# Maxima over partitions by a diagonal product in the attention part, and index tables made on VectorE

## The chip, the cores and the metric

The kernel runs on one core of a Trainium2 chip. The metric is the device time of one execution in microseconds (us). Three runs of the kernel before gave 1014.26, 1008.35 and 1012.25 us, so the median is 1012.25 us. The engines are PE (TensorE: matmuls, and PEld for its weight loads), DVE (VectorE), ACT (ScalarE), POOL (GpSimd) and SP, whose queue issues most DMAs.

## The reference

Three stages follow each other. Attention with 32 memory slots per head (4 batches, 8 heads, 576 tokens, 64 columns) gives x of 2304 tokens by 512 columns; a mixture of 8 experts, two per token, works on x; a second feed-forward of width 2048 with clipped gates gives the output.

```python
a = softmax(phi over the sequence)                 # [b, h, s, 32]
k_m, v_m = a^T k, a^T v                            # [b, h, 32, 64]
attn = softmax(q k_m^T / 8);  x = attn v_m         # [2304, 512]
logits = x @ w_gate + log1p(exp(x @ w_noise)) * noise
# top 2 experts e per token, softmax weights over the two
out[token] += weight * (relu(x[token] @ w1[e]) @ w2[e])
h = out @ w_in;  result = (h * clip(h + 3, 0, 6) / 6) @ w_out
```

## The kernel before

Attention is done in 8 groups of 4 heads (two groups make a batch; each of the 6 token columns holds 96 tokens on partitions). Per group the loads are phi (288 KB), q, k and v (576 KB each). The stages are: transposes of phi and its softmax (`stage_a1`, L502 to L516), transposes of q (`stage_q`, L524 to L534), the products with k and v (L554) and what follows from them (`stage_a2`, L560 to L587), the scores and their softmax (`stage_b`, L598 to L615, two of its steps on POOL: L604 and L613) and the product with the values (`stage_c`, L621 on POOL makes its operand `vb`, L640 is the product). After the second group of a batch its tokens are routed (`route`: some 40 small VectorE instructions and a few products).

From the routed tokens of the first batches, expert 0 starts while attention still runs (`early`: gather of token rows on POOL, L823; transposes on PE, L833; layer 1, L848; layer 2, L867). The rest of expert 0, experts 1 to 7 and the second feed-forward are part 2, in which other buffers are used.

Products in float16 need numbers within range, so several things are scaled by a power of two under their largest magnitude: per batch the values `v_m` (`us`), and each expert's w1 and w2 (`wam`). `scale_w` (L409 to L417) does that: a maximum along the row on VectorE gives one number per partition (`war`, L413), GpSimd's custom instruction PARTITION_ALL_REDUCE (L414) takes the maximum over the 128 partitions and gives it to all of them, and four small VectorE instructions make the scales (`wsm`, L416 and L389 to L394). For a batch the scale goes into `mp` (L587) and by L621 into `vb`. For weights, ScalarE and VectorE then split each of the four pieces into two halves (L403, L405); w2 of expert 0 is loaded into the same buffer as w1, once w1 is split (`st0`, one buffer, L426).

The order of all instructions is made beforehand by a planner (`Sched`): it lists every instruction with a duration, what it reads and writes and its due time, and each engine takes the one due first of those that it believes ready. On the chip each engine works through its list in that order and waits for what isn't ready. The planner counts 0.45 us for L414. Part 1 (attention and early expert 0) and part 2 are planned one behind the other.

Before the first stage constants are made: 34 warm-up products on PE, an identity matrix `ident` by `make_identity` on POOL (its second instruction, masks.py:199, is an AFFINE_SELECT), and index tables by IOTA on POOL (L316 to L325) that VectorE converts.

Of the kernel before, what the change touches and what calls it, by code (L numbers as in the profile page):

```python
# [12 lines left out]
BF16 = mybir.dt.bfloat16  # L13
# [9 lines left out]
PT = 96  # L23
# [7 lines left out]
BIG = 64  # L31
# [11 lines left out]
WARM = 34  # L43
CDMA = 1
# [3 lines left out]
def _atanh_coefs(n=5):  # L48
    """atanh(s) / s on 0 <= s <= 1/3 as a polynomial in s^2, to float32's last bit."""
# [9 lines left out]
class Buf:  # L59
    """One instance of a rotating tile, allocated when its first instruction is issued."""  # L60
# [28 lines left out]
class Sched:  # L89
    """Lists the instructions of a program with what they read and write, then issues them engine by  # L90
    engine in the order in which a list scheduler (earliest due first) would start them."""
# [71 lines left out]
    def first_due(self):  # L163
        """Latest times of all instructions if TensorE never waited."""
# [15 lines left out]
    def place(self, back):  # L180
        """List schedule by due time, from the program's start, or backwards from its end."""
# [95 lines left out]
def attn_moe_kernel(ctx, tc, q, k, v, phi, w_gate, w_noise, noise, w1, w2, w_in, w_out, out):  # L277
# [13 lines left out]
    # ---- constants  # L291
    onesh = const.tile([128, 128], F16, name="onesh")
    POOL.memset(onesh, 1.0)
    with tc.tile_pool(name="warm", bufs=1, space=bass.MemoryType.PSUM) as wp:
        pw = wp.tile([128, 128], F32, name="pw")
        for i in range(WARM):
            PE.matmul(pw, onesh, onesh, start=True, stop=True)
    ident = const.tile([128, 128], F32, name="ident")
    make_identity(nc, ident)
# [15 lines left out]
    jp = const.tile([PT, PT], I32, name="jp")  # L315
    POOL.iota(jp, pattern=[[1, PT]], base=0, channel_multiplier=-1)  # L316
    tri = const.tile([PT, PT], F16, name="tri")
    DVE.tensor_scalar(tri, jp, 0.0, None, op0=ALU.is_gt)
    toki = const.tile([PT, B * NJ], I32, name="toki")
    POOL.iota(toki.rearrange("p (b j) -> p b j", b=B), pattern=[[S, B], [1, NJ]], base=-NT // 2,  # L320
              channel_multiplier=NJ)
    tok = const.tile([PT, B * NJ], F32, name="tok")
    DVE.tensor_copy(tok, toki)
    ioi = const.tile([PT, 128], I32, name="ioi")
    POOL.iota(ioi, pattern=[[1, 128]], base=0, channel_multiplier=0)  # L325
    iof = const.tile([PT, 128], F32, name="iof")
    DVE.tensor_copy(iof, ioi)
    ef = iof[:, :NE]
    ioc = const.tile([PT, NE * NTI], F32, name="ioc")
    DVE.tensor_scalar(ioc, iof[:, :NE * NTI], float(BIG * NTI), None, op0=ALU.subtract)  # L330
    io12 = const.tile([PT, 128 + NE * NTI, 2 * NJ], F16, name="io12")
    POOL.tensor_copy(io12[:, :128], iof[:, :, None].to_broadcast([PT, 128, 2 * NJ]))
# [23 lines left out]
    # ---- tiles  # L356
# [4 lines left out]
    for pl, spec in (  # L361
            (psa, dict(da=3, oa=2)),
            (psb, dict(two=2, o3=3, o1=1)),
            (main, dict(wa=2, st0=1, xTr=1, xg=3, yt=2, wsm=6, war=2, wam=2)),
# [872 lines left out]
```

## Time and profile before

| what | us |
|---|---|
| runs, median (lowest to highest) | 1012.25 (1008.35 to 1014.26) |
| profiled execution, first to last instruction | 1015.7 |
| PE busy, share of the span | 905.2, 89% |
| DVE, ACT, POOL busy | 590.5, 452.5, 151.7 |

The profiled execution spans 1015.7 us; what lies around the span is not shown apart, so the span stands for its own time. It is 3.45 us (0.3%) above the median of the runs. In a row of a timeline the first two numbers are start and duration in us, then engine, line, operation, output and inputs with shapes; in square brackets is how long the engine was idle before it and what ended that. "issue" there means that the engine waited for nothing that the profile shows. PEclk is the granted clock of TensorE as a share of 2.4 GHz (0.5 is 1.2 GHz). A DMA share of 1 means that all 16 DMA engines were busy throughout.

### The profile page before, as it was taken

What the parts mean: (1) busy time and instruction counts of PE and PEld (TensorE: products, weight loads), DVE (VectorE), ACT (ScalarE), POOL (GpSimd) and SP (SyncE); (2) the same over time, 40 slices, a digit from 0 to 9 for tenths busy, and PEclk for the clock granted to TensorE, in tenths of its full rate; (3) what the DMA queues carried; (4) which work ended last, traced back from release to release, by engine and by line L of the source; (5) the groups of instructions that cost most, each with busy time, mean ns of one, the idle gap of its engine ahead of it and who ended that gap; (6) DMA issues with size and microseconds to landing.
All of it is one profiled execution on the core that took longest, in us unless ns stands there. A gap on an engine that the chain in (4) does not pass through costs nothing.

```text
span 1015.7 us, 14429 instructions
## 1 busy us (share of the span) xinstructions
PE 905.2 (89%) x5659; PEld 527.5 (52%) x5659; DVE 590.5 (58%) x1073; ACT 452.5 (45%) x681; POOL 151.7 (15%) x188
## 2 busy tenths in 40 slices
PE   5557447997999999898999998999999999999996
PEld 4345235564555564545565554555555555555553
DVE  1566448737979494856858536786436354343332
ACT  3365354547756273735555446544323242222322
POOL 2223233221210202020000013442001000000000
PEclk6787678997999999998999999999999999999999
DMA  9993222377997959495866423534031030200101
GB/s 227 210 253 94 52 69 85 91 279 218 293 302 233 254 169 246 169 267 160 250 227 218 151 103 113 112 99 115 10 59 43 1 71 1 52 11 2 32 1 33
DMA packets 116217, 136.45 MB, mean 134 GB/s; under 512 B 54576, under 2 KB 83248, under 8 KB 116144
## 3 DMA queue, kind: packets, MB, share of 16 engines
q1 hardware_dynamic: 109872, 115.54, 40.5%
q0 software_dynamic: 6272, 19.93, 7.4%
q8 instruction: 46, 0.75, 0.3%
q14 instruction: 27, 0.22, 0.1%
HBM read 95.26 MB, written 28.39 MB: 122 GB/s over the span
## 4 chain that ended last, share of the span: by engine, by line
PE 54%; DVE 13%; issue 11%; DMA 6%; ACT 6%; POOL 2%; SPq 1%; POOLq 0%; DVEq 0%; ACTq 0%
PE two L953 16%; PE o L977 16%; PE two L848 11%; PE o L867 8%; DMA xT<-xg 2%; DVE wa L405 2%; PE da L640 1%; DVE wb L405 1%; ACT wa L403 1%; DMA st<-moe_w_d 1%; DMA xg<-xf,ids 1%; ACT wb L403 1%; DMA ys<-yt 1%; DVE w64o L472 1%; DMA w<-moe_w_in_d 1%
## 5 line engine op out<-in xcount | busy, mean ns | idle before, releaser
L953 PE MATMUL two<-xT,wa 128*128 128x384 f16 x1152 | 196.4, 328 | 0.0
L977 PE MATMUL o<-wb,hh 128*128 128x512 f16 x864 | 194.6, 379 | 1.1 <-DVE hh L964 1.0
L953 PEld LDWEIGHTS <-wa 128*128 128x128 f16 x1152 | 113.2, 98 | 80.2 <-issue 1.7
L867 PEld LDWEIGHTS <-hh 128*128 128x128 f16 x888 | 86.7, 98 | 100.6 <-DVE hh L858 0.7
L977 PEld LDWEIGHTS <-hh 128*128 128x128 f16 x864 | 83.8, 98 | 98.4 <-DVE hh L964 2.9
L848 PE MATMUL two<-xT,wb 128*128 128x320 f16 x768 | 112.2, 308 | 8.5 <-ACT hh L856 7.6
L960 ACT ACTIVATE hf<-hf,c 128x768 f32<-128x768 f32 x48 | 44.8, 934 | 139.9 <-DVE hf L958 138.9
L867 PE MATMUL o<-wb,hh 128*128 128x512 f16 x480 | 105.9, 379 | 0.3 <-DVE hh L858 0.3
L848 PEld LDWEIGHTS <-wa 128*128 128x128 f16 x864 | 80.8, 98 | 37.2 <-issue 10.3
L958 DVE TENSOR_TENSOR hf<-two,ivb 128x768 f32<-128x768 f32 x48 | 45.8, 955 | 93.0 <-PE two L953 93.0
L848 PEld LDWEIGHTS <-wb 128*128 128x128 f16 x768 | 77.2, 101 | 43.2 <-issue 9.4
L867 PE MATMUL o<-wa,hh 128*128 128x512 f16 x408 | 90.3, 379 | 0.0
L848 PE MATMUL two<-xT,wa 128*128 128x320 f16 x576 | 80.5, 299 | 5.6 <-ACT hh L856 5.6
L640 PE MATMUL da<-vb,at 128*96 128x272 f32 x96 | 36.0, 531 | 49.2 <-POOL vb L621 25.9
L823 POOL DMA_INDIRECT xg<-xf,ids x40 | 43.7, 1092 | 199.1 <-DMA xT<-xg 171.6
L858 DVE TENSOR_TENSOR hh<-hf,hh 128x640 f16<-128x640 f32 (+1 forms) x64 | 49.2, 770 | 39.8 <-ACT hh L856 39.4
L855 ACT ACTIVATE hf<-two 128x640 f32<-128x640 f32 (+1 forms) x64 | 42.3, 661 | 60.2 <-PE two L848 60.1
L961 DVE SCALAR_TENSOR_TENSOR hh<-hf,two 128x768 f32<-128x768 f32 x48 | 45.7, 953 | 38.7 <-ACT hf L960 37.5
L964 DVE TENSOR_TENSOR hh<-hh,hh 128x768 f16<-128x768 f32 x48 | 45.9, 956 | 33.3 <-ACT hh L963 33.3
L963 ACT ACTIVATE hh<-hh 128x768 f16<-128x768 f32 x48 | 40.4, 841 | 44.4 <-DVE hh L961 44.4
L405 DVE SCALAR_TENSOR_TENSOR wb<-st,wsm,wb 128x1024 f16<-128x1024 f32 x40 | 49.4, 1281 | 7.4 <-ACT wb L403 7.3
L405 DVE SCALAR_TENSOR_TENSOR wa<-st,wsm,wa 128x1024 f16<-128x1024 f32 x40 | 49.7, 1279 | 2.9 <-ACT wa L403 2.8
(208 smaller groups left out, 1033.7 us busy)
## 6 DMA issues: line engine op xcount, KB each, us to landing
st<-moe_w_d SPq DMA_DIRECT2D x32, 1024.0 KB
ys<-yt SPq DMA_DIRECT2D x40, 256.0 KB
w<-moe_w_in_d SPq DMA_DIRECT2D x16, 512.0 KB
wf<-w64o SPq DMA_DIRECT2D x32, 256.0 KB
w<-moe_w_out_d SPq DMA_DIRECT2D x16, 512.0 KB
st<-wf SPq DMA_DIRECT2D x8, 1024.0 KB
kv<-k_d SPq DMA_DIRECT2D x8, 576.0 KB
kv<-v_d SPq DMA_DIRECT2D x8, 576.0 KB
```

The lines of the kernel that those rows point to most:

```text
L405: sch.op("DVE", dve(1024), lambda s=s, w=w, c=c: DVE.scalar_tensor_tensor(w.t[:, 1, c], s.t[:, c], sm.t[:, 2], w.t[:, 0, c], op0=ALU.mult, ...
L640: PE.matmul(po.t[:, j, :XC], at.t[:, c:c + PT], vb.t, start=True, stop=True)
L823: sch.op("POOL", 1.05, lambda t=t, xg=xg: POOL.indirect_dma_start(out=xg.t, out_offset=None, in_=xf[:rows], in_offset=bass.IndirectOffsetO ...
L848: PE.matmul(ph.t[:, i, :nw], wa.t[:, wi, c * 1024 + fb * 128:c * 1024 + fb * 128 + 128], xT.t[:, 4 * xi + c, i * nw:(i + 1) * nw], start=( ...
L858: sch.op("DVE", dve(n), lambda: DVE.tensor_tensor(hh.t[:, 1], hf.t, hh.t[:, 0], op=ALU.subtract), [hf, (hh, 0)], [(hh, 1)])
L867: PE.matmul(py.t, hs[fb].t[:, hi, tsl], wb.t[:, wi, fb * 512:(fb + 1) * 512], start=(fb == 0 and n == 0), stop=(fb == 7 and n == 2))
L953: PE.matmul(ph.t[:, i, :CW], win[fb // 8].t[:, wi, o:o + 128], xT.t[:, 4 * xi + kc, :CW], start=(n == 0), stop=(n == 11))
L958: sch.op("DVE", dve(768), lambda: DVE.tensor_tensor(t1.t, ph.t[:, :, :CW], ivb.t[:, None, :CW].to_broadcast([128, 2, CW]), op=ALU.mult), [ ...
L960: sch.op("ACT", act(768, ptr=1), lambda: ACT.activation(t1.t, t1.t, AF.Relu, bias=c3, scale=CG), [], [t1])
L961: sch.op("DVE", dve(768), lambda: DVE.scalar_tensor_tensor(gf.t, t1.t, 6.0 * CG, ph.t[:, :, :CW], op0=ALU.min, op1=ALU.mult), [t1, ph], [gf])
L964: sch.op("DVE", dve(768), lambda: DVE.tensor_tensor(g.t[:, 1], gf.t, g.t[:, 0], op=ALU.subtract), [gf, (g, 0)], [(g, 1)])
L977: PE.matmul(po[m_].t, g.t[:, gi, i, m_ * 128:(m_ + 1) * 128], wou[fb // 8].t[:, wi, (fb % 8) * 512:(fb % 8 + 1) * 512], start=(fb == 0 and ...
```

## The change

In part 1 (`sch.seg` is 0 there and 1 in part 2) `scale_w` no longer calls the custom instruction. It multiplies the identity by the column of maxima, which puts them on the diagonal of `wdg`; a product with a matrix of ones sums each column over the partitions, so that every partition holds all 128 maxima in a row of PSUM; a maximum along that row gives the same number everywhere. That holds for six calls: four batches and expert 0's w1 and w2. Part 2 keeps the custom instruction. The identity, the index tables and the token numbers are made by VectorE: a row of indices by doubling, its transpose for the partition's index, and comparisons.

```diff
+MAXPE = 0
+WLAT = (0.0, 3.0)
@@ constants
+    iof, iop, ioq = ...   # [128, 128], [128, 32], [128, 32] of float32
+    DVE.memset(iof[:, 0:1], 0.0)
+    for n in (1, 2, 4, 8, 16, 32, 64):
+        DVE.tensor_scalar(iof[:, n:2 * n], iof[:, :n], float(n), None, op0=ALU.add)
+    for i in range(4):
+        DVE.memset(ioq[32 * i:32 * i + 32], 32.0 * i)
+    DVE.transpose(iop, iof[:, :32])
+    DVE.tensor_tensor(iop, iop, ioq, op=ALU.add)
     ident = const.tile([128, 128], F32, name="ident")
-    make_identity(nc, ident)
+    DVE.tensor_scalar(ident, iof, iop[:, 0:1], None, op0=ALU.is_equal)
...
-    POOL.iota(jp, pattern=[[1, PT]], base=0, channel_multiplier=-1)
-    DVE.tensor_scalar(tri, jp, 0.0, None, op0=ALU.is_gt)
+    DVE.tensor_scalar(tri, iof[:PT, :PT], iop[:PT, 0:1], None, op0=ALU.is_gt)
-    POOL.iota(toki...); DVE.tensor_copy(tok, toki); POOL.iota(ioi...); DVE.tensor_copy(iof, ioi)
+    DVE.tensor_scalar(p6, iop[:PT, 0:1], float(NJ), float(-NT // 2), op0=ALU.mult, op1=ALU.add)
+    for b in range(B):
+        DVE.tensor_scalar(tok[:, b * NJ:(b + 1) * NJ], iof[:PT, :NJ], p6, float(S * b), op0=ALU.add, op1=ALU.add)
@@ def scale_w
+        if sch.seg <= MAXPE:
+            wd, px = new("wdg", [128, 128], BF16), new(PS[sch.seg][2], [128, 128])
+            sch.op("DVE", 0.15, lambda: DVE.tensor_scalar(wd.t, identb, ar.t[:, 0], None, op0=ALU.mult), [(ar, 0)], [wd],
+                   lat=WLAT[sch.seg])
+            sch.op("PE", 0.06, lambda: PE.matmul(px.t, onesb, wd.t, start=True, stop=True), [wd], [px], lat=0.12)
+            sch.op("DVE", dve(128), lambda: DVE.tensor_reduce(ar.t[:, 1], px.t, axis=AX.X, op=ALU.max), [px], [(ar, 1)])
+            pow2_ops(...)   # as before
+            return sm
         sch.op("POOL", 0.45, lambda: POOL.partition_all_reduce(...), [(ar, 0)], [(ar, 1)])
```

The planner makes its order anew, so instructions of part 1 change places; in part 2 nearly all stay. Three places show it. Lines of the changed kernel are 16 higher from L414 on (L613 is L629 there, L848 is L864).

On POOL, around the first batch's maximum (`war`), the order before was this; an ISA row stands where the engine's code is set for the instruction behind it:

```order
L604 TENSOR_TENSOR sc_352<-sc_352,sm_359 128x576
L414 ISA
L414 ISA war_382<-war_382 128x1
L613 ISA
L613 TENSOR_TENSOR sc_352<-sc_352,sm_359 128x576
L621 TENSOR_TENSOR vb_356<-kd_283,mp_455 128x256
L621 TENSOR_TENSOR vb_441<-kd_366,mp_455 128x256
```

and now it is this, from the first instruction of the softmax on:

```order
L620 ISA
L620 TENSOR_TENSOR sc_367<-sc_367,sm_370 128x576
L629 TENSOR_TENSOR sc_367<-sc_367,sm_370 128x576
L637 TENSOR_TENSOR vb_338<-kd_294,mp_474 128x256
L620 TENSOR_TENSOR sc_472<-sc_472,sm_476 128x576
L637 TENSOR_TENSOR vb_445<-kd_377,mp_474 128x256
```

The reduction and both settings of code around it are gone, and one setting stands ahead of the first softmax instead.

On VectorE, at the program's start, conversions of POOL's tables stood ahead of the first maximum of phi (`st`, from `da` in PSUM):

```order
L301 CAST identh<-ident 128x128
L303 CAST identb<-ident 128x128
L318 TENSOR_SCALAR tri<-jp 96x96
L323 CAST tok<-toki 96x24
L327 CAST iof<-ioi 96x128
L509 TENSOR_REDUCE st_216<-da_205 128x1
```

Now VectorE builds the tables (the first rows, with five doublings, are left out here):

```order
L306 TENSOR_SCALAR iof<-iof 128x32
L309 STREAM_TRANSPOSE iop<-iof 128x32
L306 TENSOR_SCALAR iof<-iof 128x64
L337 TENSOR_SCALAR ioc<-iof 96x40
L310 TENSOR_TENSOR iop<-iop,ioq 128x32
L312 TENSOR_SCALAR ident<-iof,iop 128x128
L329 TENSOR_SCALAR tri<-iof,iop 96x96
L314 CAST identh<-ident 128x128
```

The identity is VectorE's own fourteenth row and waits for no other engine.

On PE, where group 6's product with the values (`da` from `vb`) meets expert 0's early start, the last transpose of gathered tokens (`xg`), the product and layer 1 (with `wa`, w1's halves) followed each other:

```order
L833 LDWEIGHTS xg_1384
L833 MATMUL oa_1463<-identh,xg_1384 128x128
L640 MATMUL da_1473<-vb_1194,at_1445 96x272 x2
L848 LDWEIGHTS wa_1429
L848 MATMUL da_1492<-xTe_1456,wa_1429 128x256
```

Now w2's diagonal `wdg` has its product there:

```order
L656 MATMUL da_1459<-vb_1245,at_1454 96x272 x2
L656 MATMUL da_1464<-vb_1245,at_1454 96x272 x2
L656 MATMUL da_1494<-vb_1245,at_1454 96x272 x2
L426 LDWEIGHTS onesb
L426 MATMUL oa_1559<-wdg_1557,onesb 128x128
L849 LDWEIGHTS xg_1361
L849 MATMUL oa_1561<-identh,xg_1361 128x128
```

The product for w2's maximum stands ahead of all transposes of the gathered tokens and of layer 1; before, neither of them stood behind w2's maximum on PE.

## Rows read from the trace of the kernel before

**Rows 1.** Busy time by stretch, as the columns in the first row say.
```profile
core 0: us, PE busy (x) PEld busy (x) DVE busy (x) ACT busy (x) POOL busy (x), PEclk, DMA share, GB/s
...
30.00:45.00 15.00, 3.30 (x25) 2.17 (x26) 4.92 (x14) 3.21 (x6) 2.62 (x4) 0.68 1.08 243
...
80.00:103.00 23.00, 20.51 (x163) 14.88 (x162) 18.27 (x65) 14.55 (x30) 8.21 (x8) 0.78 0.31 86
103.00:119.00 16.00, 2.51 (x58) 1.78 (x54) 5.98 (x28) 2.01 (x4) 1.58 (x5) 0.63 0.27 63
...
156.00:208.00 52.00, 45.84 (x376) 32.07 (x376) 40.58 (x124) 28.38 (x66) 15.51 (x20) 0.94 0.31 100
208.00:1015.70 807.70, 773.57 (x4440) 432.06 (x4438) 473.30 (x696) 354.56 (x488) 91.88 (x96) 0.98 0.47 134
```

**Rows 2.** Waits up to 200 us: who, for whom; total, times, longest.
```profile
...
PEld da L640 <- POOL vb L621: 50.1, 4, 14.1
```

**Rows 3.** Timeline of POOL: start, duration, engine, line, tiles; idle time before.
```profile
...
11.04 0.28 POOL masks.py:199 TENSOR_SCALAR_AFFINE_SELECT ident<-ident 128x128 f32<-128x128 f32 x1 [9.82 <-issue]
...
35.20 0.41 POOL L414 PARTITION_ALL_REDUCE war<-war  x1 [6.19 <-issue]
42.79 1.15 POOL L613 TENSOR_TENSOR sc<-sc,sm 128x576 f32<-128x576 f32 x1 [7.19 <-issue]
43.91 1.41 POOL L621 TENSOR_TENSOR vb<-kd,mp 128x256 f32<-128x256 f32 x2
```

**Rows 4.** Timeline of PE: the matmuls behind its longest idle times.
```profile
...
11.37 1.22 PE L507 MATMUL da<-ident,phr 96*128 96x96 f32 x6 [6.57 <-POOL ident masks.py:199]
...
44.90 5.05 PE L640 MATMUL da<-vb,at 128*96 128x272 f32 x12 [11.22 <-DVE at L615]
...
79.53 3.90 PE L640 MATMUL da<-vb,at 128*96 128x272 f32 x8 [12.10 <-POOL vb L621]
...
119.33 2.12 PE L640 MATMUL da<-vb,at 128*96 128x272 f32 x4 [13.82 <-POOL vb L621]
...
155.77 3.91 PE L640 MATMUL da<-vb,at 128*96 128x272 f32 x8 [12.04 <-DVE at L615]
```

**Rows 5.** Timeline of DVE: the chains around the first three maxima.
```profile
...
28.36 0.29 DVE L568 TENSOR_REDUCE us<-kd 128x1 f32<-128x128 f32 x1
28.68 0.15 DVE L413 TENSOR_REDUCE war<-us 128x1 f32<-128x2 f32 x1
...
62.36 0.10 DVE L413 TENSOR_REDUCE war<-us 128x1 f32<-128x2 f32 x1
...
101.64 0.09 DVE L413 TENSOR_REDUCE war<-us 128x1 f32<-128x2 f32 x1
...
111.22 0.34 DVE L587 TENSOR_SCALAR mp<-maskp,wsm 128x256 f32<-128x256 f32 x1
```

**Rows 6.** Timeline of PE: the products of groups 2 and 3 that use k and v.
```profile
...
49.88 1.52 PE L554 MATMUL oa<-kv,e 96*32 96x128 f32 x48
...
58.76 1.52 PE L554 MATMUL oa<-kv,e 96*32 96x128 f32 x48
```

**Rows 7.** Expert 0: POOL, SP, DMA from 168 to 170 us, PE.
```profile
...
146.16 0.76 POOL L414 PARTITION_ALL_REDUCE war<-war  x2 [7.05 <-issue]
...
161.84 0.95 SPq L426 DMA_DIRECT2D st<-moe_w_d  x2
...
168.00:170.00 2.00, 2.00 (x27) 1.84 (x24) 1.97 (x6) 1.49 (x7) 0.39 (x1) 1.00 0.52 199
...
162.63 2.78 PE L848 MATMUL da<-xTe,wa 128*128 128x256 f16 x24 [0.48 <-ACT xv L646]
...
177.78 0.41 POOL L414 PARTITION_ALL_REDUCE war<-war  x1 [5.89 <-DVE hhe L858]
...
182.45 7.93 PE L867 MATMUL oa<-wa,hhe 128*128 128x512 f16 x36
```

**Rows 8.** One line of VectorE: duration ns min/median/max, first and last start.
```profile
...
L703 DVE SCALAR_TENSOR_TENSOR gt<-gt,iof x8: 196/204/1203, 85.2 to 192.3; 96x48 f32<-96x48 f32 x8
```

More of the change, by code (lines that the diff above doesn't have):

```diff
@@ L8 @@
 from concourse.bass import ds
-from concourse.masks import make_identity
 from concourse._compat import with_exitstack
@@ L297, in attn_moe_kernel @@
             PE.matmul(pw, onesh, onesh, start=True, stop=True)
+    iof = const.tile([128, 128], F32, name="iof")
+    iop = const.tile([128, 32], F32, name="iop")
+    ioq = const.tile([128, 32], F32, name="ioq")
+    DVE.memset(iof[:, 0:1], 0.0)
[5 more added lines that the diff above has]
+    DVE.tensor_tensor(iop, iop, ioq, op=ALU.add)
     ident = const.tile([128, 128], F32, name="ident")
-    make_identity(nc, ident)
+    DVE.tensor_scalar(ident, iof, iop[:, 0:1], None, op0=ALU.is_equal)
     identh = const.tile([128, 128], F16, name="identh")
@@ L314, in attn_moe_kernel @@
         POOL.memset(maskp[32 * h:32 * h + 32, h // 2, :], 1.0)
-    jp = const.tile([PT, PT], I32, name="jp")
-    POOL.iota(jp, pattern=[[1, PT]], base=0, channel_multiplier=-1)
     tri = const.tile([PT, PT], F16, name="tri")
-    DVE.tensor_scalar(tri, jp, 0.0, None, op0=ALU.is_gt)
-    toki = const.tile([PT, B * NJ], I32, name="toki")
-    POOL.iota(toki.rearrange("p (b j) -> p b j", b=B), pattern=[[S, B], [1, NJ]], base=-NT // 2,
-              channel_multiplier=NJ)
+    DVE.tensor_scalar(tri, iof[:PT, :PT], iop[:PT, 0:1], None, op0=ALU.is_gt)
     tok = const.tile([PT, B * NJ], F32, name="tok")
[L323 to L328, printed above, removed]
+    p6 = const.tile([PT, 1], F32, name="p6")
+    DVE.tensor_scalar(p6, iop[:PT, 0:1], float(NJ), float(-NT // 2), op0=ALU.mult, op1=ALU.add)
+    for b in range(B):
+        DVE.tensor_scalar(tok[:, b * NJ:(b + 1) * NJ], iof[:PT, :NJ], p6, float(S * b), op0=ALU.add, op1=ALU.add)
+    ef = iof[:PT, :NE]
     ioc = const.tile([PT, NE * NTI], F32, name="ioc")
-    DVE.tensor_scalar(ioc, iof[:, :NE * NTI], float(BIG * NTI), None, op0=ALU.subtract)
+    DVE.tensor_scalar(ioc, iof[:PT, :NE * NTI], float(BIG * NTI), None, op0=ALU.subtract)
     io12 = const.tile([PT, 128 + NE * NTI, 2 * NJ], F16, name="io12")
-    POOL.tensor_copy(io12[:, :128], iof[:, :, None].to_broadcast([PT, 128, 2 * NJ]))
+    POOL.tensor_copy(io12[:, :128], iof[:PT, :, None].to_broadcast([PT, 128, 2 * NJ]))
     POOL.tensor_copy(io12[:, 128:], ioc[:, :, None].to_broadcast([PT, NE * NTI, 2 * NJ]))
@@ L363, in attn_moe_kernel @@
             (psb, dict(two=2, o3=3, o1=1)),
-            (main, dict(wa=2, st0=1, xTr=1, xg=3, yt=2, wsm=6, war=2, wam=2)),
+            (main, dict(wa=2, st0=1, xTr=1, xg=3, yt=2, wsm=6, war=2, wam=2, wdg=2)),
             (att, dict(xTe=2, hhe=8, hfe=2, ph=2, kv=2, qt=2, phr=1, qr=1, st=3, aT=1, e=1, kd=3, kT=2, vb=3, qT=1, sc=2, sm=2, at=2,
```

1 line of the change is left out of this document (added).

## The prediction, made before the changed kernel ran

> **What bounds the kernel.** I read the table by stretch first. From 208 us to the end PE is busy for 773.6 of 807.7 us at 0.98 of the full clock [rows 1]: part 2 is bound by TensorE, and the change leaves its instructions alone. Part 1 is another matter. From 30 to 45 us PE works for 3.3 us, from 103 to 119 for 2.5 us [rows 1]. So I read PE's timeline next: five idle times stand out, 6.57 us ahead of the first transposes, then 11.22, 12.10, 13.82 and 12.04 us, each of the last four ahead of a product with the values [rows 4]. The list of waits gives their releaser: PE's weight loads waited 50.1 us in four times for `vb` of POOL's L621 [rows 2]. POOL's timeline says why: it is idle for 6.19 us ahead of the first PARTITION_ALL_REDUCE, which takes 0.41 us, and for 7.19 us behind it, both put down to "issue", and only then come L613 and the two L621 [rows 3]. The reader is to see one pattern, which stands four times in the trace, once for each batch: a maximum of 0.41 us costs POOL some 14 us, and PE stands still. The order shows what the idle times are: an ISA row ahead of the custom instruction and one behind it, a change of POOL's code. At the start it is the same, 9.82 us of "issue" ahead of the AFFINE_SELECT that makes the identity [rows 3].
>
> **The change part by part.** *Start.* The identity now waits for no code. VectorE's chain to it has about 14 small instructions; a small dependent one takes 0.10 to 0.15 us [rows 5], and I allow 0.2 us each with the hand-over, so 2.8 us and `ident` at about 4 us instead of 11.3. The first transposes cannot start before PE's warm-up ends, at 4.80 us (11.37 less 6.57 [rows 4]), nor before phi's copy on ACT, which is late next; I take 5.4 us. Gain 6 us by itself, between 4 and 6.5. The tables for routing also leave POOL; their VectorE instructions lie in the same idle time.
>
> *What replaces the custom instruction.* Added per maximum: one multiplication of 128 x 128 (nearest row the 128 x 256 `mp`, 0.34 us), one product of 128 columns, one maximum along 128 columns (nearest row L568, 0.29 us) [rows 5], and three hand-overs between engines. I take 1.2 us; the bounds are 0.7 us (the durations alone) and 2.5 us, if each instruction waits for one of up to 0.7 us ahead of it. VectorE and PE have the time in these places.
>
> *First batch.* `war` is there at 28.83 us [rows 5]. Then 1.2 us for the product, `mp` of 0.34 us and one L621 of 0.70 us [rows 3, 5], and between them in VectorE's order the four small instructions, two maxima over pieces of w1 and three steps of the softmaxes, for which I allow 5.8 us: `vb` at 36.9 us in the old time, against 44.87: 8 of the 11.2 us go. With the start that would be 14 us. But here the loads come in. From 30 to 45 us the DMA engines are full, at 243 GB/s [rows 1], and what is queued up to the values of group 3 is, by the sizes of the tensors, 10.76 MB: 44.3 us at that rate, so they are there at about 46 us, however early the engines are free. Group 3's product stood at 58.76 us, group 2's at 49.88 [rows 6]. So the first two gaps together cannot give more than 12.8 us at this place. I take 12.5, between 9 and 14.5.
>
> *Second batch.* `war` at 62.46 us [rows 5], plus 1.2 us, four small instructions, `mp` and L621: `vb` at about 67 us. PE has its own products until 67.4 us (79.53 less 12.10 [rows 4]). The gap of 12.1 us closes. It comes back in part: in a gap VectorE does work of its own (5.98 us from 103 to 119 us, of which I count 4 us as work that other engines did not wait for), and behind the gap it is busy for 18.27 of 23 us [rows 1], so that 4 us still fit, hardly. In return PE is cold behind each gap, a clock of 0.78 over the 23 us [rows 1]. Together I put this at a loss of 1 us, from a gain of 2 to a loss of 4: 11.1 us.
>
> *Third batch.* `war` at 101.73 us [rows 5]; nine instructions of the routing stand between the parts of the chain, so `vb` at about 107 us against 119.33, with 105.5 us as PE's own end [rows 4]. The gap falls by 12.3 us; the backlog on VectorE is larger and I take off 2: 10.3 us, between 7 and 13.5.
>
> *Fourth gap: a wait takes its place.* This is the step where I part from a plain sum. In the new order the product for w2's maximum stands ahead of the token transposes and of layer 1. What it waits for is a chain: w1's maximum (before: 146.16 us), split of w1, load of w2 into the same buffer (issue 161.84 us, the DMA engines only half busy with it from 168 to 170), its sums, then the maximum (177.78 us) [rows 7]. Without the change of code ahead of w1's maximum (7.05 us [rows 7]), and without the one behind it (7.19 us at the first batch [rows 3]), which held L613 and so VectorE's part of the split, the load can be issued some 13 of these 14 us sooner, at 149 us of the old time. It lands 7 to 8 us later, and with 1.2 us for the last sum and 1.2 us for the product w2's maximum is there at about 159 us. PE has nothing else from about 144 us on (155.77 less 12.04 [rows 4]). Then two sets of transposes and copies, so that layer 1 starts at 162 us; before, it started at 162.63 [rows 7]. Layer 1 then runs 2.5 us cold, but the wait for layer 2's weights goes, whose products started at 182.45 us [rows 7]: by the same durations they start at 180.2. So of the 12.04 us only 2.3 us are kept, between a loss of 3 and a gain of 7.
>
> *Part 2.* Its instructions and nearly all their order stay, and its first custom instruction still needs one change of code. All of it moves forward as a whole: 0, give or take 3 us.
>
> Sum: 12.5 + 11.1 + 10.3 + 2.3 = 36.2 us off the profiled span of 1015.7 us, so 979.5; that span stands 3.45 us above the median of the runs, so I predict 976 us.
>
> The Trainium skill speaks against this change in one place: its page "GPSIMD Engine Reference", section 4.1 (Engine selection), gives reductions over partitions to GpSimd, and makes no exception for small ones. By the 0.41 us of the instruction alone it would be right here, and the change would gain nothing but the start, the rival without change below: 1006 us. The same page, section 2.1 (Instruction dispatch), says that the first call of freshly loaded code pays some 6 us for loading. The trace agrees with that one: 6.19 and 7.19 us [rows 3]; the two sections taken together speak for the change wherever calls alternate with ordinary instructions.
>
> **Rivals.** *Less, by VectorE and GpSimd getting in each other's way.* L703, a VectorE instruction of 0.20 us, took up to 1.20 us [rows 8]. I read that as a wait for POOL's access to the same memory. With the gaps gone both work side by side for more of the time. If each of POOL's some 50 two-input instructions of part 1 held VectorE for 0.25 us more, 12 us would go: 988 us. Against it: by the median of 0.20 most calls are not hit. The Trainium skill has this as a rule ("SBUF — State Buffer", section Who interferes with whom): a VectorE instruction with two inputs in SBUF and a GpSimd instruction that reads SBUF block each other for a whole instruction. The row fits it, in its size.
>
> *More.* If w2's maximum is there sooner, because the split runs in one piece, or PE's clock stays up, the fourth gap goes as well: 36.2 - 2.3 + 12 = 46 us, 966 us.
>
> *No change.* The code changes belong to ordinary instructions too, or turn up ahead of other ones, so that only the start gains, 1006 us at best, or the loads refill the gaps. Against it: each 7 us of idle time stands beside a custom instruction, and loads rest (DMA share 0.27 from 103 to 119 us [rows 1]).
>
> *Slower.* The wait for w2 at the new place decides everything. If the loads refill the three first gaps, so that w1's maximum comes no earlier than its 146.6 us, layer 1 starts 31 us (w1's maximum to w2's before [rows 7]) and 3 us later, at 181 instead of 162.6 us, and layer 2 at 198 instead of 182.45: 15.6 us more, 1028 us. It turns to a loss once w1's maximum comes later than about 131 us. I expect it at about 107 us.
>
> **How the numbers follow.** Within 0.5%, 5 us, is about what a measurement here cannot tell from no change. Forecast (968 to 985 us) 0.60; less (985 to 1005) 0.16; more (950 to 968) 0.17; no change 0.04; slower 0.03. Faster is then 0.93. The ends of the four terms and of part 2 all at once give 13 to 50 us; that they fall together is unlikely. Leaving out a tenth on either side, the range is 959 to 992 us.
>
> **What would show it.** In the new profile the first transposes start near 5.5 us; POOL has no idle time of 6 us or more put down to issue from 20 us until part 2; the product of group 3 stands at 46 to 48 us; the third batch's product with the values starts at 83 to 86 us; PE is idle for some 10 us or more ahead of the product L426 for w2, at about 125 us; layer 2 starts at about 146 us, and part 2 takes as long as before, to 3 us. It would be wrong if the code change ahead of L620 at the start takes until the first softmax needs it (about 20 us), if VectorE is full and PE's gaps merely move, or if PE's wait for w2 is much shorter or longer.

## The result and the profile after

The changed kernel takes 982.62 us (median of 4 runs, 977.03 to 985.13) against 1010.31 us before (4 runs, 1008.35 to 1014.26): a ratio of 0.9723, 95% interval 0.9681 to 0.9766. The gain is 27.7 us; 36.2 us were predicted, with a time of 976 us and a range of 959 to 992. The profiled span fell from 1015.7 to 982.1 us, by 33.6 us; the two figures differ because the profiled execution of before was longer than its runs (its span alone is 5.4 us over their median), while that of after took 984.29 us, 1.7 over its median.

First the stretches of the changed kernel, as in [rows 1].

```profile
core 0: us, PE busy (x) PEld busy (x) DVE busy (x) ACT busy (x) POOL busy (x), PEclk, DMA share, GB/s
...
24.00:40.00 16.00, 8.26 (x89) 5.55 (x81) 12.96 (x30) 8.56 (x15) 4.85 (x5) 0.82 1.08 249
40.00:64.00 24.00, 22.08 (x229) 15.43 (x233) 13.38 (x41) 17.44 (x32) 8.32 (x8) 0.82 1.09 262
64.00:100.00 36.00, 29.35 (x305) 21.39 (x295) 35.06 (x139) 23.96 (x48) 15.52 (x19) 0.95 0.59 155
100.00:119.00 19.00, 13.71 (x104) 9.16 (x102) 14.98 (x36) 11.26 (x21) 8.89 (x10) 0.83 0.32 92
119.00:132.00 13.00, 0.69 (x4) 0.27 (x3) 12.28 (x39) 5.69 (x11) 6.05 (x8) 0.55 0.43 162
...
178.00:982.10 804.10, 772.85 (x4440) 431.99 (x4438) 473.01 (x696) 355.02 (x488) 95.14 (x96) 0.98 0.47 135
```

The long holes in PE's work are gone from 24 to 119 us; the one that is left lies from 119 to 132 us, where PE works for 0.69 of 13 us. From 64 to 100 us VectorE is busy for 35.06 of 36 us: that is what the removed gaps uncovered. Up to 64 us the DMA engines are full. Part 2 took 804.25 us from its first row at 177.85 us, against 807.87 from 207.83.

GpSimd's timeline, in answer to [rows 3]:

```profile
...
33.74 0.72 POOL L637 TENSOR_TENSOR vb<-kd,mp 128x256 f32<-128x256 f32 x1 [2.13 <-DVE mp L603]
...
60.81 1.41 POOL L637 TENSOR_TENSOR vb<-kd,mp 128x256 f32<-128x256 f32 x2 [2.04 <-DVE mp L603]
...
88.08 1.43 POOL L637 TENSOR_TENSOR vb<-kd,mp 128x256 f32<-128x256 f32 x2 [2.35 <-DVE mm L716]
...
160.97 0.49 POOL L827 TENSOR_TENSOR gwt<-mk,fac 96x48 f32<-96x48 f32 x2 [7.74 <-issue]
...
197.56 0.41 POOL L430 PARTITION_ALL_REDUCE war<-war  x1 [8.24 <-issue]
```

The products `vb` of the first three batches (L637) come after 2.0 to 2.4 us of idle time, which VectorE's results end, where before 7.19 us of issue stood behind the first custom instruction. The setting of code ahead of the first softmax instruction (L620) stands at 6.5 us, and L620 waits for VectorE until 25.11 us, so it is hidden. The wait of 7.74 us at 160.97 us bears the word "issue", but no ISA row stands ahead of it: the factors that it multiplies by come from VectorE at 160.8 and 161.0 us. The next change of code is the one with 8.24 us ahead of the first PARTITION_ALL_REDUCE of part 2; a gather stands 0.19 us behind that instruction, so there no second one is paid. The wait in [rows 2], 50.1 us for four, is one of 2.7 us now.

PE, in answer to [rows 4, 6, 7]: the first transposes, the products with the values of the four batches, those with k and v of groups 2 and 3, w2's maximum, layers 1 and 2, and the start of part 2.

```profile
...
5.28 0.71 PE L523 MATMUL da<-ident,phr 96*128 96x96 f32 x6 [0.69 <-ACT phr L518]
...
34.51 1.75 PE L656 MATMUL da<-vb,at 128*96 128x272 f32 x4 [2.57 <-POOL vb L637]
...
40.02 2.79 PE L570 MATMUL oa<-kv,e 96*32 96x128 f32 x48 [3.76 <-DMA kv<-v_d]
...
52.62 1.52 PE L570 MATMUL oa<-kv,e 96*32 96x128 f32 x48
...
64.50 1.84 PE L656 MATMUL da<-vb,at 128*96 128x272 f32 x7
...
89.28 1.08 PE L656 MATMUL da<-vb,at 128*96 128x272 f32 x4
...
113.74 2.04 PE L656 MATMUL da<-vb,at 128*96 128x272 f32 x8 [2.24 <-DVE at L631]
...
132.46 0.27 PE L426 MATMUL oa<-wdg,onesb 128*128 128x128 bf16 x1 [12.76 <-DVE wdg L424]
...
136.10 4.21 PE L864 MATMUL da<-xTe,wa 128*128 128x256 f16 x19
...
152.97 7.30 PE L883 MATMUL oa<-wa,hhe 128*128 128x512 f16 x33
...
177.85 2.34 PE L864 MATMUL two<-xTr,wa 128*128 128x256 f16 x20 [1.24 <-ACT xTr L851]
```

Part 2 of the kernel before starts with this row:

```profile
...
207.83 4.42 PE L848 MATMUL two<-xTr,wa 128*128 128x256 f16 x39 [1.24 <-ACT xTr L835]
```

The reader is to subtract: 11.37 - 5.28 = 6.1 us at the start, 10.4 at the first product with the values, 9.9 at group 2's product and 6.1 at group 3's, 15.0 at the second batch's, 30.1 at the third batch's, 42.0 at the fourth's, 26.5 at layer 1, 29.5 at layer 2, 30.0 at the start of part 2. So the whole gain is there at 89 us; the fourth gap gives 12 us more, and the 12.76 us ahead of L426, the new wait that was forecast, take them back.

VectorE around the first maximum, around w1's and at w2's last sum, in answer to [rows 5], and SP's issue of w2's load:

```profile
...
26.54 0.15 DVE L420 TENSOR_REDUCE war<-us 128x1 f32<-128x2 f32 x1
26.73 0.25 DVE L424 TENSOR_SCALAR wdg<-identb,war 128x128 bf16<-128x128 bf16 x1
...
30.21 0.23 DVE L427 TENSOR_REDUCE war<-oa 128x1 f32<-128x128 f32 x1
...
33.35 0.31 DVE L603 TENSOR_SCALAR mp<-maskp,wsm 128x256 f32<-128x256 f32 x1
...
108.41 1.25 DVE L603 TENSOR_SCALAR mp<-maskp,wsm 128x256 f32<-128x256 f32 x1
109.58 1.82 DVE L676 TENSOR_TENSOR L<-L,xv 96x32 f32<-96x32 f32 x1
111.33 0.28 DVE L427 TENSOR_REDUCE war<-oa 128x1 f32<-128x128 f32 x1
...
113.87 4.87 DVE L412 SCALAR_TENSOR_TENSOR wa<-st,wsm,wa 128x1024 f16<-128x1024 f32 x4 [0.27 <-ACT wa L410]
...
118.77 0.95 SPq L442 DMA_DIRECT2D st<-moe_w_d  x2
...
130.65 1.21 DVE L452 TENSOR_REDUCE wam<-st 128x1 f32<-128x1024 f32 x1
```

The first maximum takes 3.9 us from `war` to its result, through PE and back, behind a maximum over a piece of w1 and four other instructions; the next three take 2.1, 1.9 and 3.6 us. At the fourth, an `mp` of 0.31 us takes 1.25 and an L676 of 0.17 us takes 1.82, while GpSimd runs three instructions with two inputs one behind the other; w1's maximum waits for them until 111.33 us, its split ends at 118.7, and SP issues w2's load right behind it, at 118.77 us (before: 161.84 [rows 7]). The last packet of that load ends at 126.9 us, but VectorE, which is busy for 12.28 of the 13 us from 119 to 132 us, takes up its maximum over the last piece of w2 (L452) only at 130.65 us. PE's product for w2 comes right behind that.

### The profile page after: what moved, and what is told of

Same layout as the page of the kernel before. It is cut to its first block, busy times and chain, and to the rows that moved or that the text cites. A ratio compares the mean times of both kernels' runs of the same rounds, so it can differ in the third digit from the quotient of the medians.

```text
span 982.1 us, 14437 instructions
## 1 busy us (share of the span) xinstructions
PE 907.1 (92%) x5665; PEld 529.2 (54%) x5665; DVE 595.1 (61%) x1103; ACT 454.0 (46%) x681; POOL 151.9 (15%) x177
## 4 chain that ended last, share of the span: by engine, by line
PE 71%; DVE 9%; DMA 8%; ACT 5%; issue 3%; SPq 2%; POOL 1%; POOLq 0%; DVEq 0%; ACTq 0%
PE two L969 18%; PE o L993 18%; PE two L864 16%; PE o L883 12%; DMA wf<-w64o 2%; PE da L864 2%; DMA ph<-phi_d 2%; DMA st<-moe_w_d 1%; ACT wb L410 1%; PE oa L883 1%; PE da L656 1%; DMA xT<-xg 1%; DMA xg<-xf,ids 1%; DMA yb<-ys,slot 1%; POOL xg L839 1%
## 5 line engine op out<-in xcount | busy, mean ns | idle before, releaser
L864 PE MATMUL two<-xT,wb 128*128 128x320 f16 x768 | 108.6, 302 | 1.8 <-ACT hh L872 1.0
L864 PEld LDWEIGHTS <-wa 128*128 128x128 f16 x864 | 82.6, 100 | 35.8 <-issue 7.0
L864 PEld LDWEIGHTS <-wb 128*128 128x128 f16 x768 | 75.8, 99 | 34.3 <-issue 2.5
L864 PE MATMUL two<-xT,wa 128*128 128x320 f16 x576 | 82.5, 304 | 5.5 <-ACT hh L872 5.5
L839 POOL DMA_INDIRECT xg<-xf,ids x40 | 46.2, 1155 | 207.9 <-DMA xT<-xg 167.8
L452 DVE TENSOR_REDUCE wam<-st 128x1 f32<-128x1024 f32 x40 | 47.5, 1211 | 6.2 <-DMA st<-moe_w_d 6.0
```

The source lines that it names most:

```text
L452: sch.op("DVE", dve(1024), lambda i=i: DVE.tensor_reduce(am.t[:, i:i + 1], s.t[:, i * 1024:(i + 1) * 1024], axis=AX.X, op=ALU.max, apply_a ...
L839: sch.op("POOL", 1.05, lambda t=t, xg=xg: POOL.indirect_dma_start(out=xg.t, out_offset=None, in_=xf[:rows], in_offset=bass.IndirectOffsetO ...
L864: PE.matmul(ph.t[:, i, :nw], wa.t[:, wi, c * 1024 + fb * 128:c * 1024 + fb * 128 + 128], xT.t[:, 4 * xi + c, i * nw:(i + 1) * nw], start=( ...
```

## The experiments

All runs were compared with the kernel before on the same chip; its medians in the later comparisons were 1011.73, 1012.49 and 1011.87 us. The table has the places that tell the kernels apart: the products with the values of the second and third batch, layer 2, the start of part 2 (us in the profiled execution) and what follows from there to the end.

| kernel | median us | ratio (95%) | 2nd | 3rd | layer 2 | part 2 | its length |
|---|---|---|---|---|---|---|---|
| before | 1010.31 | | 79.53 | 119.33 | 182.45 | 207.83 | 807.9 |
| changed | 982.62 | 0.972 (0.968 to 0.977) | 64.50 | 89.28 | 152.97 | 177.85 | 804.3 |
| start alone | 1003.27 | 0.992 (0.990 to 0.995) | 74.12 | 111.65 | 175.25 | 200.74 | 800.6 |
| maxima alone | 978.09 | 0.968 (0.962 to 0.974) | 63.91 | 88.68 | 149.61 | 174.50 | 803.2 |
| one more custom instruction | 991.38 | 0.981 (0.977 to 0.986) | 65.76 | 102.84 | 164.52 | 189.39 | 800.0 |
| w2 behind layer 1 | 977.20 | 0.966 (0.962 to 0.970) | 62.45 | 87.06 | 142.44 | 169.10 | 806.4 |
| ... and third tile behind layer 2 | 970.43 | 0.958 (0.954 to 0.963) | 61.18 | 89.56 | 139.35 | 167.34 | 803.9 |
| w1 loaded later | 983.54 | 0.972 (0.968 to 0.976) | 62.90 | 91.31 | 153.15 | 178.04 | 801.6 |
| all three moves | 973.43 | 0.963 (0.958 to 0.967) | 61.45 | 88.82 | 137.85 | 165.84 | 804.8 |
| product in part 2 too | 990.08 | 0.980 (0.975 to 0.986) | 59.85 | 85.81 | 147.92 | 172.81 | 813.8 |
| less VectorE | 987.58 | 0.976 (0.973 to 0.980) | 64.83 | 95.34 | 160.54 | 185.42 | 806.8 |
| more VectorE | 985.62 | 0.974 (0.970 to 0.978) | 62.94 | 94.95 | 154.71 | 179.60 | 807.4 |
| both w2 moves, less VectorE | 979.15 | 0.969 (0.965 to 0.973) | 60.20 | 90.68 | 143.39 | 171.37 | 805.5 |

One reading comes ahead of the others. Part 2 holds the same instructions in all rows but one (the product in part 2), and takes 800.0 to 807.9 us there, with no order in it. The 3.6 us that part 2 seems to gain between the two profiles are within this spread, so the change is to be read from part 1.

### One custom instruction more

```
-        ar = new("war", [128, 2, 1])
+        ar = new("war", [128, 3, 1])
...
+            if len(T["wdg"].made) == 2:
+                sch.op("POOL", 0.45, lambda: POOL.partition_all_reduce(ar.t[:, 2], ar.t[:, 0], channels=128,
+                                                                       reduce_op=RED.absmax), [(ar, 0)], [(ar, 2)])
             wd, px = new("wdg", [128, 128], BF16), new(PS[sch.seg][2], [128, 128])
```

> The changed kernel with one PARTITION_ALL_REDUCE more, in the third batch, at the place where the maximum was taken before; nothing reads its result. If it is the change of code that costs, POOL shows idle time of 6 to 7 us put down to issue ahead of it and again behind it, the third batch's product with the values is 10 to 14 us later than 89.3 us, with a PE gap of some 10 us, and the time is 990 to 996 us. If it was the wait for the result (the chain over the custom instruction), an unread one costs nothing: 981 to 984 us.

Measured 991.38 us, 8.8 more than the changed kernel (the intervals of the two ratios just touch), and the third batch's product 13.6 us later; 1.3 of these were there at the second batch's product, up to which both kernels have the same order. GpSimd and PE of this kernel:

```profile
...
94.68 0.41 POOL L424 PARTITION_ALL_REDUCE war<-war  x1 [7.68 <-issue]
102.07 1.40 POOL L640 TENSOR_TENSOR vb<-kd,mp 128x256 f32<-128x256 f32 x2 [6.98 <-issue]
```

```profile
...
102.84 1.68 PE L659 MATMUL da<-vb,at 128*96 128x272 f32 x3 [12.15 <-POOL vb L640]
```

Nobody reads what the instruction computes, and it takes 0.41 us; GpSimd stands still for 7.68 us ahead of it and for 6.98 behind it, and PE for 12.15 us. VectorE had the custom instruction's input ready at 86.4 us and L640's, `mp`, at 89.2 us, so neither idle time is a wait for data; an ISA row stands at the start of each. So the change of code is the price, and it is paid twice. This is the same 14 us as in [rows 3], put back by one instruction. The Trainium skill's "GPSIMD Engine Reference", section 2.1, has some 6 us for the first call of freshly loaded code; the trace agrees in kind, with 7.68 us, and shows 6.98 us once more on the way back to an ordinary instruction. Its section 4.1, which gives reductions over partitions to GpSimd, is not borne out in part 1: there the product with ones, of 0.23 us on PE, was the cheaper way.

### The two halves apart

Start alone:

```
-MAXPE = 0
+MAXPE = -1
```

Maxima alone, with the tables as before the change too:

```
-    DVE.tensor_scalar(ident, iof, iop[:, 0:1], None, op0=ALU.is_equal)
+    make_identity(nc, ident)
...
+    POOL.iota(jp, pattern=[[1, PT]], base=0, channel_multiplier=-1)
...
+    POOL.iota(ioi, pattern=[[1, 128]], base=0, channel_multiplier=0)
```

> The start alone: identity and tables on VectorE, all maxima by the custom instruction. Theory of the prediction (gains of the start are kept until the loads bind, and the loads do not bind with the long gaps still there): first transposes at 5.3 us as in the changed kernel, every later stage of part 1 earlier by about 6 us, the four gaps of 11 to 14 us ahead of the products with the values all there, 1010.3 - 6 = 1004 us (1001 to 1007). Rival, the loads take the start back already in the first batch: the product of group 2 at 48 to 50 us as before, no gain, 1010 us.

> The maxima alone: diagonal product in part 1, identity and tables made by GpSimd as before the change. If the two halves of the change simply add up, the 6.1 us of the start are missing from the 27.7 us measured: 988.7 us. Theory of the prediction (loads cap what the first batch can give): a start that is 6 us later removes PE's wait of 3.8 us for the values of group 2, so only some 2 us are missing: 983 to 986 us, with group 2's product at 40 to 42 us and no wait for a load ahead of it.

The start alone gives 1003.27 us, as forecast; its four gaps are all there, though the first three are shorter than the 11 to 14 us of the forecast (8.07, 10.78, 10.69 and 12.60 us). Two of them:

```profile
...
40.56 5.72 PE L656 MATMUL da<-vb,at 128*96 128x272 f32 x12 [8.07 <-DVE at L631]
...
74.12 3.65 PE L656 MATMUL da<-vb,at 128*96 128x272 f32 x8 [10.78 <-POOL vb L637]
```

The maxima alone give 978.09 us, less than the whole change (the intervals overlap). I had expected 983 to 986, and the simple sum 988.7. PE of this kernel:

```profile
...
10.71 1.22 PE L520 MATMUL da<-ident,phr 96*128 96x96 f32 x6 [5.91 <-POOL ident masks.py:199]
...
40.45 1.94 PE L567 MATMUL oa<-kv,e 96*32 96x128 f32 x32 [3.80 <-DMA kv<-v_d]
```

The first transposes stand 5.4 us later than in the changed kernel, group 2's product only 0.4 us later: the loads have taken the difference. But the wait for the values is still there, 3.80 us, where I had expected none. So beside the product for the maxima the start has no measurable worth: 7.8 us alone (0.77% of 1011.7), nothing together. The loads' place at 40 us is a reason for it, and half of my mechanism (no wait any more) was wrong. It is not the only difference: the granted clock over part 1 was 0.91 in this execution and 0.83 in the changed kernel's, and what that is worth was not tried.

### The loads of the first 64 us

The load of w1, 2.1 MB that are needed only at 104 us, is made to wait in the planner's list for the values of group 3, and then stands behind those of group 4 on SP:

```
-                590e3, w=[(kv, i)])
+                590e3, w=[(kv, i)] + ([hold] if g == 3 and i else []))
...
-                1 << 20, w=[(s, 2 * i), (s, 2 * i + 1)])
+                1 << 20, after, [(s, 2 * i), (s, 2 * i + 1)])
...
+        a, sa = load_w(w1[e].rearrange("(c p) f -> p c f", p=128), "st0", tg, after=[] if e else [hold])
```

> The changed kernel with the load of expert 0's first weights (2.1 MB, about 8 us at 264 GB/s) issued behind group 4's keys and values instead of ahead of group 2's. Theory (full DMA engines, not the engines of the core, hold the first batch: PE waits 3.8 us for the values of group 2 at 40.0 us): no wait for a load ahead of group 2's product, which moves from 40.0 to about 36 us, the second batch's product with the values from 64.5 to 59 to 61 us, and the time falls by 3 to 6 us, to 977 to 980 us. Rival (PE's own order and VectorE hold these stages, so the loads only fill time that is lost anyway, and w1's four sums of 1.2 us now fall where VectorE is full): the second batch's product stays at 63 to 65 us and the time at 981 to 985 us.

983.54 us: no gain. PE of this kernel, the products of groups 2 and 3 and the second batch's product with the values:

```profile
...
30.53 2.14 PE L572 MATMUL oa<-kv,e 96*32 96x128 f32 x48
...
46.79 1.52 PE L572 MATMUL oa<-kv,e 96*32 96x128 f32 x48
...
62.90 1.39 PE L658 MATMUL da<-vb,at 128*96 128x272 f32 x5
```

Group 2's product comes 9.5 us earlier, without a wait for a load, group 3's 5.8 us, the second batch's product 1.6 us and the third batch's 2.0 us later. The wait for group 2 was real, and of the 9.5 us 1.6 were left thirty microseconds on and none at the third batch. What loads that land sooner go with is shown by another pair. The kernel with the product in part 2 too (below) has the same instructions in the same order as the changed kernel on all engines up to part 2. In its execution the loads were sooner:

```profile
...
35.68 2.79 PE L570 MATMUL oa<-kv,e 96*32 96x128 f32 x48 [2.24 <-DMA kv<-v_d]
...
48.80 1.52 PE L570 MATMUL oa<-kv,e 96*32 96x128 f32 x48
...
59.85 2.07 PE L656 MATMUL da<-vb,at 128*96 128x272 f32 x8
```

Against 40.02 and 64.50 us group 2's product is 4.3 us earlier and the second batch's 4.7; at the third batch 3.5 us are left, at the start of part 2 5.0. ScalarE saw the same: its wait for group 2's queries ended at 38.06 us there, and here at 42.68. The first row is of that kernel, the other two are of the changed one:

```profile
...
38.06 1.58 ACT L540 ACTIVATE qr<-qt 96x768 f32<-96x768 f32 x2 [3.46 <-DMA qt<-q_d]
...
23.84 1.58 ACT L540 ACTIVATE qr<-qt 96x768 f32<-96x768 f32 x2 [4.11 <-DMA qt<-q_d]
...
42.68 1.58 ACT L540 ACTIVATE qr<-qt 96x768 f32<-96x768 f32 x2 [5.72 <-DMA qt<-q_d]
```

Two executions of the same part 1 differ by 5 us. The difference grows over the waits for loads and then stays: 0.3 us at group 0's values (11.85 and 11.53 us), 2.6 at group 1's queries, which were issued at 9.0 and 9.2 us and used at 23.84 and 21.20, 4.3 at group 2's values. The DMA engines were full in both and moved 249 against 260 GB/s from 24 to 40 us, 262 against 278 from 40 to 64. So a place in part 1, read from one profile, is good to some 5 us. I take this for the main part of the scatter of 8 us among the changed kernel's runs; that every run scatters for this reason was not tried, and their granted clocks differ too (0.956 to 0.968).

### The wait for w2's maximum

The place of w2's product in PE's order is set by the program's list: the tiles `oa` are handed out in its order. In the first kernel w2 (`load_second`) comes in the list behind the gather of the first two token tiles (`W2AT = (0, 0, 7)`), in the second the third tile's gather also moves behind layer 2:

```
-            W[0] = load_expert(0)
+            first = load_first(0)
+            W[0] = first[:1]
...
                 (early, early1, early2)[f](i)
+            if (f, i, s) == W2AT:
+                W[0] = load_second(0, *first)
```

```
-EAT = ((2, 1, 12), (0, 1, 9), (1, 1, 10), (0, 0, 7), (1, 0, 8), (2, 0, 9))
+EAT = ((2, 1, 12), (2, 0, 9), (0, 1, 9), (1, 1, 10), (0, 0, 7), (1, 0, 8))
```

> The changed kernel with the product for w2's maximum placed seven blocks of layer 1 later in PE's order (w2 is loaded and scaled behind the token transposes in the program's list). Theory (PE's 12.8 us of idle time ahead of that product is a wait that the new order made, and nothing else is late there): layer 1 starts at 119 to 122 us instead of 136.1, the product stands at 131 to 135 us with under 3 us of idle time ahead of it, layer 2 starts at 139 to 144 us instead of 153.0, and the time falls by 8 to 12 us to 971 to 975 us. Rival (w2's split or the transfers behind it set layer 2 anyway, or part 2 waits for the last batch's tokens): layer 2 or part 2 stays where it is, 980 to 984 us.

> The changed kernel with w2's product behind layer 1 (as in the run before, 977.2 us) and, further, the transposes of the third early token tile behind layer 2 of the first two, where they stood ahead of it and made PE wait 7.0 us for a gather at 141.6 us. Theory (that wait took the place of w2's): layer 2 starts at 136 to 140 us instead of 142.4, no idle time over 3 us ahead of it, and the time falls by 2 to 5 us against 977.2, to 972 to 975 us. Rival (w2's split on VectorE, which ended at 139.6 us, sets layer 2, and the third tile is needed at the same time as before): layer 2 at 141 to 143 us, 976 to 979 us.

977.20 and 970.43 us. PE of the first:

```profile
...
116.54 10.41 PE L870 MATMUL da<-xTe,wa 128*128 128x256 f16 x84
128.81 0.22 PE L427 MATMUL oa<-wdg,onesb 128*128 128x128 bf16 x1 [1.85 <-DVE wdg L425]
...
141.61 1.03 PE L855 MATMUL oa<-identh,xg 128*128 128x128 f16 x8 [6.96 <-DMA xg<-xf,ids]
142.44 7.77 PE L889 MATMUL oa<-wa,hhe 128*128 128x512 f16 x27
```

Layer 1 starts at 116.54 us instead of 136.10, w2's product waits 1.85 us instead of 12.76. Layer 2 starts 10.5 us earlier, where layer 1 gained 19.6: a new wait of 6.96 us for a gather stands ahead of it, which no theory of mine had named, and the time misses its forecast of 971 to 975 us. The second kernel takes that wait away. Its PE:

```profile
...
118.56 11.00 PE L870 MATMUL da<-xTe,wa 128*128 128x256 f16 x84 [2.11 <-ACT xv L668]
...
139.35 5.96 PE L889 MATMUL oa<-wa,hhe 128*128 128x512 f16 x19
```

Layer 2 at 139.35 us, the forecast of this run, and the fastest kernel of the study: 0.9581 of before (0.9537 to 0.9625), which does not overlap with the changed kernel's interval. So the new wait of the fourth gap was worth about 12 us of time, and could be had by changes in the order alone: 5.4 us by w2's move and the rest with the third tile's. The third tile's move by itself was not tried. All three moves together:

> The three moves together: w1's load behind group 4's values, w2's product and the third tile's transposes behind layer 1 and layer 2. If the loads hold the first stages and PE's order the last, the gains add up: 982.6 less 5 less 8 to 10 gives 967 to 970 us. If one of them only moves the wait to another place, no better than the better of the two: 972 to 977 us.

973.43 us, no better than without w1's move, as after the run on w1.

### VectorE between 64 and 100 us

Less: four of the tiles go by ScalarE and GpSimd (`LO`, places 6, 9, 11 and 13 from D to P). More: each row maximum of groups 2 to 4 is taken three times.

```
-LO = "DPPPDDDPPDPDPDPPPDPPPPDD"
+LO = "DPPPDDPPPPPPPPPPPDPPPPDD"
```

```
+        if g in (2, 3, 4):
+            for _ in range(2):
+                sch.op("DVE", dve(576), lambda: DVE.tensor_reduce(sm.t[:, 0], sc.t, axis=AX.X, op=ALU.max), [sc], [(sm, 0)])
```

> The changed kernel with less VectorE work in the second and third batch: four tiles of the value products (groups 2 to 4) go by ScalarE's copy and GpSimd's subtraction instead of VectorE's, some 0.85 us less of VectorE each, 3.4 us in all. Theory (from 64 to 100 us VectorE, busy for 35.1 of 36 us, is what the removed gaps uncovered, and sets the pace): the third batch's product with the values moves from 89.3 to 86 to 87 us and the time falls by 2 to 4 us, to 979 to 981 us. Rival (the DMA engines, full until 70 us, or PE's own order set it): 88.5 to 90 us, and 981 to 985 us.

> The changed kernel with more VectorE work in the second and third batch: for groups 2 to 4 each maximum along a row of the softmax is taken three times instead of once, six instructions of 0.74 us, 4.4 us in all; the result stays the same. Theory (VectorE sets the pace there): the third batch's product with the values moves from 89.3 to 92.5 to 94 us, the time rises by 3 to 5 us, to 986 to 988 us. Rival (VectorE waits for the loads or for PE in between and has the room): 89 to 91 us, 982 to 984 us.

> The fastest version so far (w2's product behind layer 1, the third token tile's transposes behind layer 2, 970.4 us) with the same four tiles taken off VectorE. If VectorE sets the pace of the second and third batch, 966 to 969 us; if not, 969 to 972 us.

More work puts the third batch's product from 89.28 to 94.95 us, as the theory has it; but of the six instructions only four lie ahead of that product, 2.9 us for a shift of 5.7. Less work puts it to 95.34 us, against the theory. The times of these two, 985.62 and 987.58 us, cannot be told from the changed kernel's (the intervals overlap); on top of the fastest kernel less work costs 8.7 us, clear of the noise. ScalarE of the kernel with less:

```profile
...
72.38 0.62 ACT L662 ACTIVATE xv<-da 96x544 f32<-96x544 f32 x1 [1.73 <-DVE L L673]
...
84.39 0.63 ACT L662 ACTIVATE xv<-da 96x544 f32<-96x544 f32 x1 [2.43 <-DVE cnt L762]
```

The tiles `xv` of that way are two. The first of these waits is ended by VectorE's copy L673, which reads such a tile and stands behind routing work in VectorE's order, and PE then waits 2.87 us for ScalarE; the second is ended by a copy of the routing itself, L762. Nor did VectorE have less to do in the stretch: from the second batch's product to the third's it is busy for 24.0 us in the changed kernel, 25.8 with less and 29.0 with more, for other work of its own moved in. So the three runs do not show that VectorE's amount of work sets the pace from 64 to 100 us. From the second batch's product to the third's the changed kernel takes 24.8 us, the one with less VectorE work 30.5, the one with more 32.0, and the planner orders the stretch anew in both. What limits it stays open.

### The product in part 2 too

```
-MAXPE = 0
+MAXPE = 1
```

> The changed kernel with the diagonal product in part 2 as well, so that no custom instruction is left there. Theory (part 2 is bound by PE, at 0.98 of the full clock, and its changes of code lie beside PE's work): 0 to 2 us less, 980 to 984 us, and PE's wait of 6.3 us at 206.9 us, which ACT's copies of the gathered tokens end, stays over 4 us. Rival (the first change of code, 8.2 us of issue ahead of 197.6 us, holds up the gathers behind it on POOL, and so that wait): PE's wait falls under 2 us, 975 to 979 us.

990.08 us, and part 1 was even 5 us shorter in the profile: part 2 takes 813.8 us, 6 to 14 more than in the other kernels. Both forecasts of the time were wrong. The wait of 6.3 us did go, as the rival had it (ScalarE's copies of the gathered tokens now end 1.1 us at most), but others came in its place, 4.0 us for a maximum and 4.1 for two gathers among them. In all PE is idle for 37.5 us of part 2, against 31.2 in the changed kernel. One wait stands out (engine, line, who for whom; us in total, times, longest):

```profile
...
PE o L939 <- ACT xg L926: 9.3, 1, 9.3
```

In the changed kernel the same wait, ahead of the second feed-forward's transposes, is 2.1 us. The planner had put part 2 in another order for the new instructions; whether the product or that order costs the time was not taken apart.

## Why the prediction was right, and where its sum was not

- **The pattern.** Right: the custom instruction costs GpSimd a change of code on either side, and PE waits for it. One instruction put back brings 14.7 us of idle time and 12.15 us for PE.
- **The start.** Right in place (5.28 us, forecast 5.4). As a gain by itself it was 7.8 us, above the forecast of 6 and its upper end of 6.5, but the interval reaches from 5 to 10.5. Right too that it cannot be added to the rest.
- **The product in place of the custom instruction, 1.2 us.** It was too low: 3.9, 2.1, 1.9 and 3.6 us in the four batches, twice beyond the bound of 2.5. The whole way from `war` to `vb` in the first batch took 7.8 us all the same, 8.0 forecast.
- **The first batch, 12.5 us by the loads' cap.** This is the step that failed. It read "are there at about 46 us" for group 3 and took group 3's product as the place where the cap binds. That stood at 52.62 us, with no wait for a load; the loads bound group 2 instead, whose values held PE until 40.02 us and whose queries held ScalarE until 42.68. Then the chain from group 2 to group 3 was still to run, 12.6 us where it had been 8.9, with PE busy for 12.3 us of it instead of 7.7. In two other kernels with the same order here (the product in part 2 too, one more custom instruction) group 2's product stood at 35.68 and 42.37 us, after waits of 2.24 and 5.94 us for its values, and group 3's 13.1 and 12.3 us behind it. So the place was wrong in all three, while the size goes with the loads: 6.1 us instead of 12.5 here, outside the bounds, and 10.0 where they came soonest, inside them. w1's load moved away from group 2 gave nothing in the end, loads that all came earlier gave 5 us.
- **The second batch, 11.1 us.** 15.0 - 6.1 = 8.9 us, within the bounds. Both together, 15.0 against 23.6, are the shortfall.
- **The third batch, 10.3 us.** 30.05 - 15.03 = 15.02 us, beyond the upper bound of 13.5: the gap of 13.82 us went, and the backlog on VectorE that I had charged with 2 us cost nothing at this place. In sum 30.1 of 33.9 us.
- **The fourth gap, 2.3 us.** 30.0 - 30.1: nothing was kept. The mechanism is as predicted: PE waits for w2 at the new place, for 12.76 us (10 or more forecast), and moving that product gave 5.4 us back, 12.2 with the third tile's move. Two things made the size. Of the 7 us by which layer 2 missed its 146 us, 3.8 are what the first three terms lacked. The rest lies between w2's load and its maximum: the load was issued at 148.9 us of the old time (118.77 + 30.1; 149 forecast) and landed 8.1 us later (7 to 8 forecast), but the last maximum over w2 stood behind VectorE's own work until 130.65 us, so that w2's product came 13.7 us after the issue instead of 10. That VectorE's order is the reason is read from the rows; no run changed it alone. For "runs 2.5 us cold" the prediction names no row: the first 4.65 us of layer 1 ran at a granted clock of 0.50 and the rest at 1.00, which makes about 2.3 us (an estimate, half of 4.65).
- **Part 2, 0 give or take 3 us.** 3.6 us between the two profiles; the spread over kernels with the same part 2 is 8 us.
- **Rival "less", GpSimd and VectorE blocking each other.** It is there, but not as a new loss. I added up by how much the VectorE instructions of the first 170 us exceed the median of their kind and shape over all the kernels here, as L703 did in [rows 8]: some 14 us before, 12 after. The two rows at 108 to 111 us above are among the largest. The Trainium skill's "SBUF — State Buffer", section Who interferes with whom, says that a VectorE instruction with two inputs there contends with a GpSimd instruction that reads there, and that `tensor_scalar` can too; the two rows agree with it (1.82 and 1.25 us, while GpSimd works without a break).
- **Why the time was still within the range.** The shortfall of 8.6 us in the first two batches and 2.4 in the fourth was met by 4.7 more in the third; of the 36.2 us, 30.0 stand in part 1. In the execution with the sooner loads (the kernel with the product in part 2 too) the same order gives 10.0, 9.7, 13.8 and 1.5 us, 35.0 in sum, with group 3's product at 48.80 us, the third batch's at 85.81 and layer 2 at 147.92, close to the signs that were named. So how near the single terms come is partly luck of the execution; the failed place in the first batch and the late maximum of w2 are in both. The time of 982.62 us is 6.6 over the forecast: 2.6 are missing from the span (33.6 of 36.2, of which 3.6 in part 2 are within its spread), and the 3.45 us taken off for the profile of before did not hold for the one of after, whose span of 982.1 us lies 0.5 below the median of the runs. The ends of the terms add up to some 18 to 52 us, not 13 to 50; the range does not rest on them.

## What to carry to other kernels

A short custom instruction on GpSimd between ordinary ones is priced by the idle time on both sides of it, not by its own: look at "issue" ahead of it and behind it, and replace it where calls alternate with ordinary instructions. In part 2, where it stood among gathers and beside full work of PE, replacing it gained nothing here. When a gap goes, ask at the next three places what is late there (loads, another engine's backlog, a product whose place in an in-order queue was fixed by the program's list), and do not add the gains of edits that meet at the same late load. The wait that the new order made was the largest thing left, and two moves in the program's list took 12 us out of it.

## What the runs showed that I had not expected

- The same instructions of part 1 took 177.85 and 172.81 us in two executions, with loads that landed 4 us apart at 40 us, with the DMA engines full in both (shares of 1.07 to 1.10).
- Moving 3.4 us of work off an engine that was busy for 97% of a stretch made the stretch 5.7 us longer: in the new order that engine had 1.8 us more to do there, not less, and ScalarE waited for a buffer of two that it frees.
- Part 2 took between 800.0 and 807.9 us with the same instructions, so that a gain of 4 us in it cannot be read from one profile.
